# Exponentials of the first softmax transposed on VectorE, and the product with v in 32x32 tiles

## The chip, the cores and the metric

The kernel runs on one core of one Trainium2 chip. Its time is the device time of one execution in microseconds, given as the median of several executions. A core has TensorE (PE, with PEld for the loads of its stationary operand, the "weights"), VectorE (DVE), ScalarE (ACT), GpSimd (POOL), which here mostly issues loads, and SyncE (SP), which issues the output transfers. Each engine works through its own list of instructions in order; they wait for each other by semaphores.

## What is computed

Batch 8, 8 heads, 576 positions, head size 64, 32 packed rows. Two attentions follow each other, then a layer of two matrices with a squared ReLU between:

```python
def sm_attn(qq, kk, vv):
    s = scale * np.matmul(qq, kk.transpose(0, 1, 3, 2))
    s = s - np.max(s, axis=-1, keepdims=True)
    a = np.exp(s)
    a = a / (np.sum(a, axis=-1, keepdims=True) + 1e-09)
    return np.matmul(a, vv)
p_packed = sm_attn(p, k, v)              # 32 rows per head over 576 keys
out = sm_attn(q, p_packed, p_packed)     # 576 rows per head over 32 keys
x = out.transpose(0, 2, 1, 3).reshape(8 * 576, 512)
result = np.maximum(x @ w_in, 0) ** 2 @ w_out     # w_in 512x2048, w_out 2048x512
```

## The kernel before

Work is cut by batch b (0 to 7) and by quad qd (two groups of four heads). Four heads of 32 packed rows fill the 128 partitions.

For each batch and quad: k (and q) are loaded by POOL with a cast to bf16 as 128 rows of 18 positions x 64 (`load_rows`, L265 to L272; for batches 2 to 7, `WIDE`, in two halves of positions, and turned by some multiples of 32 partitions, which makes two transfers of one) and transposed in 32x32 blocks by VectorE into kT (`st_k`, L353). `st_s1` makes the first scores on PE in 32x32 tiles (`scores`, L377): four heads on four rows and columns of tiles, each head's 64 dimensions as two steps e. VectorE takes the negated maximum (L403), ScalarE the exponentials e1 with their sums (L415). Then e1 has to be turned so that keys lie on partitions: `st_e1T` (L435) does it on PE, in 128x128 transposes into PSUM, five a quad in batches 2 to 7 and six 96-row ones in batches 0 and 1 (`THREES`, whose scores are cut in thirds), and `st_e1T_out` copies the result to SBUF on VectorE or ScalarE (L421, L423). `st_pv` (L459) multiplies by v: 5 or 6 steps of keys, four heads in four column tiles, 64 columns each. v is loaded for it in another layout than k, `load_v` (L310, L315, L316), keys 4 or 6 in a row. Results are scaled by the reciprocal of the sums (L446, L472), transposed in two ways (ppd by VectorE, L480; ppT by PE, L498), and ppd is shifted by 64 partitions (`st_shift`) for the second attention.

The second attention: scores s2 (L377), transposed by VectorE (L517, L520), maximum, subtraction, exponentials, sums, normalization (L525 to L551) and transposition to a2T (L565). The first layer is folded into the packed rows: wp = ppT x w_in (L576, "w" words, copied out by "W" words), and h = wp x a2T (L592), relu (L597, L599), square into gT (L635, L637), and the second layer o (L650), which is copied out and sent by SP (L681).

The order is written out by hand: `ORDER` is a string of words, each a step, which are issued in that order; every engine gets its instructions in the order of the words. A word names a step, batch, quad or blocks, and after a colon the engine (v VectorE, a ScalarE, p POOL). `Lk00` loads k of batch 0 quad 0, `LA0`/`LB0` two parts of q of batch 0, `Wi11` a part of w_in, `Wo0` a part of w_out; `s100` scores, `m100` maximum, `x100` exponentials, `eT00` transposes, `eo00` their copy, `rd`, `pv`, `pp`, `bd`, `bs`, `pt`, `po` the steps around the product with v; `zA`, `tA`, `mA`, `sA`, `xA`, `uA`, `aA`, `TA` (and B) the second softmax of batches 0 and 1 in two parts of positions, `s2`, `t2`, ... `aT` that of the later ones; `h`, `r`, `q`, `o`, `c`, `d` the layers; `Z30` thirty dummy matmuls (`busy`, L337), which keep PE running while it waits at the start. `p_first` and `p_cast` load and turn p of batches 0 and 1; `Pr`, `Px`, `Pt`, `Pu` do it for the others, `Pu` being a copy of pT turned by 64 partitions, for the second half of the scores.

Of the kernel before, what the change touches and what calls it, by code (L numbers as in the profile page):

```python
# [29 lines left out]
THREES = range(2)  # L30
# [8 lines left out]
THIRDS = ((0, S // 3), (S // 3, S // 3 * 2), (S // 3 * 2, S))  # L39
# [11 lines left out]
pf Lk00 Lk01 Lv00 LA0 Lv01 Wi11 P0 Wi10 kT00 I Z30 s100 Wi00 LB0 kT01 P1 Wi01 m100 Z7 s101 Wi21 x100 m101 x101 Z6 eT00  # L51
Wi20 qA01 Z1 eT01 qA00 eo00:a eo01:v Lk10 rd0 Z5 pv0 pp0 bd0 Z3 pt0 Lk11 zA0 po0:v tA01 tA00 Z10 wb00 mA01 Wb00:a mA00
Z2 wb01 sA01:p Wb01:v Wo0 sA00:v xA01 uA01 xA00 Lv11 qB00 qB01 aA01:p uA00 Z21 zB0 Lv10 tB01 Z1 wa00 tB00 aA00:p mB01
Wa00:a Z1 wa01 TA01 mB00 Wa01:a sB01:p TA00 sB00:v Z5 h0.0.8 xB01 h0.0.1 xB00 r0.0.8:v h0.0.0 Wo2 r0.0.1:a h0.0.3 uB01
r0.0.0:a h0.0.10 uB00 h0.0.11 aB01:p r0.0.10:a h0.0.2 r0.0.3:a q0.0.0:v r0.0.2:a h0.0.9 r0.0.11:v aB00:p q0.0.1:a TB01
w101 LA1 q0.0.5:v r0.0.9:a w100 TB00 W101:a W100:v h0.1.0 q0.0.4:p h0.1.1 h0.1.11 r0.1.0:a h0.1.10 r0.1.1:a kT10
h0.1.2 r0.1.10:a LB1 h0.1.3 r0.1.11:a h0.0.12 r0.1.2:a q0.1.0:v h0.1.15 r0.1.3:a q0.1.5:p h0.0.4 r0.0.12:v r0.1.15:a
h0.0.13 kT11 r0.0.4:a h0.1.6 h0.0.5 r0.0.13:a Wo1 h0.0.6 q0.1.1:v r0.1.6:a h0.1.13 q0.0.6:v r0.0.5:a s11 r0.1.13:v Wo3
q0.0.2:a r0.0.6:v h0.1.14 m110 h0.1.7 r0.1.14:a h0.1.12 Pr h0.1.9 r0.1.7:a h0.1.4 q0.1.7:v r0.1.12:a h0.0.15 r0.1.9:v
x110 h0.0.14 r0.1.4:v h0.0.7 m111 r0.0.15:a h0.1.8 eT10 r0.0.14:a r0.1.8:v h0.1.5 r0.0.7:a o2.0 eo10:v q0.1.3:a o3.0  # L60
r0.1.5:v x111 q0.0.3:v o1.0 q0.1.2:v o0.0 q0.1.4:a q0.0.7:v o0.1 rd1 q0.1.6:p eT11 o1.1 eo11:v o3.1 pv1 Lk20 o0.2 pp1
o1.2 bd1 o3.2 o1.3 qA10 pt1 qA11 o0.3 o3.3 po1:v zA1 qB11 w011 tA11 o2.1 W011:a tA10 o2.2 qB10 o2.3 mA11 mA10 w110
w111 sA11 o3.4 Lk21 W110:a sA10 o1.4 W111:v o0.4 xA11 o0.5 xA10 uA11 zB1 w010 tB11 o1.5 uA10 o1.6 aA11 W010:a o0.6
mB11 o1.7 aA10 o2.4 Px TA11 Lk30 c1:v o3.5 o0.7 TA10 sB11 o3.6 kT20 d1 c0:a h1.0.8 Lv20 o2.5 r1.0.8:a Pt h1.0.3 xB11
h1.0.6 tB10 d0 r1.0.3:a o2.6 Pu:v h1.0.1 r1.0.6:a Lv21 o2.7 r1.0.1:a kT21 h1.0.0 c2:a h1.0.2 o3.7 r1.0.0:a uB11 Lv30
d2 r1.0.2:a s12 q1.0.0:v c3:a h1.0.4 mB10 o4.0 m120 q1.0.1:a Lq2 h1.0.5 d3 o5.0 r1.0.4:a m121 r1.0.5:a o5.1 aB11 x120
h1.0.12 q1.0.2:v h1.0.7 o4.1 kT30 Lq3 x121 eT20 o4.2 TB11 r1.0.12:a r1.0.7:v o5.2 sB10 eo20:a h1.0.13 rd2 q1.0.3:v
eT21 xB10 r1.0.13:v h1.0.9 eo21:a o4.3 r1.0.9:v h1.0.15 q1.0.6:a uB10 pv2 q1.0.4:v h1.0.10 pp2 o5.3 Lv31 r1.0.15:a
r1.0.10:v o4.4 aB10 pt2 h1.0.14 bd2 h1.0.11 po2:v r1.0.14:a o5.4 bs2:v r1.0.11:a w121 TB10 w020 q1.0.5:v W121:a h1.1.8
q1.0.7:v h1.1.9 o4.5 W020:v o5.5 r1.1.8:a r1.1.9:a o4.6 Lv40 h1.1.4 qT21 h1.1.6 r1.1.4:a o5.6 q1.1.4:a qT20 o4.7 Lk31  # L70
r1.1.6:a h1.1.2 o5.7 c4:v h1.1.14 r1.1.2:a s22 c5:a r1.1.14:v h1.1.10 t221 o6.0 d5 r1.1.10:a h1.1.1 t220 o6.1 r1.1.1:a
h1.1.7 m221 o6.2 d4 h1.1.0 r1.1.7:a o6.3 qT30 r1.1.0:a h1.1.5 q1.1.3:a h1.1.3 q1.1.0:v Lq4 o6.4 qT31 r1.1.5:a o6.5
q1.1.2:a sb21:v h1.1.13 r1.1.3:a o8.0 m220 r1.1.13:a h1.1.11 o6.6 q1.1.1:a Lq5 r1.1.11:v o6.7 x221 sb20:v h1.1.15 o8.1
c6:a q1.1.5:v h1.1.12 x220 su21 d6 o7.0 r1.1.12:a Lk41 w120 r1.1.15:a w021 kT31 q1.1.6:a o7.1 q1.1.7:a o8.2 su20
W120:a o7.2 o8.3 a221 W021:a o7.3 a220 o8.4 o7.4 aT21 o8.5 aT20 o7.5 h2.0.2 h2.0.3 r2.0.2:v o7.6 Lk40 r2.0.3:a o8.6
q2.0.1 o7.7 h2.0.1 h2.0.0 r2.0.1:v o8.7 r2.0.0:a c7:v s13 c8:a q2.0.0 h2.0.7 d7 h2.0.6 m130 Lk50 r2.0.7:a o9.0
r2.0.6:a h2.0.4 m131 o10.0 d8 r2.0.4:a h2.0.9 q2.0.3 x131 h2.0.5 r2.0.9:v o10.1 r2.0.5:v x130 o9.1 kT41 h2.0.12
h2.0.10 r2.0.12:a q2.0.2 eT31 Lk51 r2.0.10:a eT30 rd3 h2.1.1 eo31:v h2.0.8 r2.1.1:a o9.2 kT40 r2.0.8:a h2.1.0 eo30:a
o9.3 r2.1.0:v h2.0.11 Lk60 q2.0.4 pv3 q2.1.0 r2.0.11:a h2.1.3 pp3 o10.2 r2.1.3:a q2.0.5 h2.0.13 bd3 o10.3 bs3:v
r2.0.13:a Lv41 h2.1.5 h2.0.14 r2.1.5:v s23 q2.0.6 o9.4 qT40 r2.0.14:a h2.0.15 o9.5 t231 r2.0.15:a h2.1.4 h2.1.8 q2.0.7  # L80
o10.4 Lv51 r2.1.8:a t230 o9.6 r2.1.4:a o10.5 m231 h2.1.7 h2.1.2 q2.1.2 o9.7 r2.1.7:a qT41 r2.1.2:a o10.6 c9:a sb31:v
h2.1.11 Lq6 h2.1.14 r2.1.11:a d9 o11.0 q2.1.1 h2.1.6 m230 r2.1.14:a o11.1 r2.1.6:a o10.7 x231 sb30:v h2.1.10 h2.1.12
q2.1.3 pt3 r2.1.10:a o11.2 c10:v po3:a h2.1.9 r2.1.12:a su31 w030 x230 w130 d10 o11.3 r2.1.9:a q2.1.5 W030:a o12.0
q2.1.4 h2.1.13 su30 o12.1 W130:a o11.4 a231 o12.2 r2.1.13:a w131 a230 w031 o12.3 W031:a aT31 o11.5 aT30 h2.1.15 W131:v
o12.4 r2.1.15:a h3.0.0 h3.0.11 r3.0.0:a o12.5 q2.1.6 q2.1.7 r3.0.11:a h3.0.1 s14 r3.0.1:v h3.0.3 kT51 h3.0.7 r3.0.3:a
o11.6 r3.0.7:a m140 h3.0.10 o11.7 r3.0.10:a q3.0.0 h3.0.8 x140 kT50 h3.0.2 o12.6 r3.0.8:a c11:v o12.7 Lk61 r3.0.2:a
h3.0.14 q3.0.5 h3.0.5 d11 m141 o14.0 r3.0.14:a c12:a eT40 q3.0.1 h3.0.4 r3.0.5:a o13.0 x141 r3.0.4:v Lk71 h3.1.9 d12
eo40:v o14.1 r3.1.9:a q3.0.2 o13.1 h3.0.12 rd4 h3.0.6 o13.2 r3.0.12:v r3.0.6:a o14.2 h3.0.13 q3.0.3 h3.1.8 eT41
r3.0.13:v o13.3 r3.1.8:a eo41:v h3.0.9 q3.0.6 h3.0.15 o14.3 q3.1.4 r3.0.9:a r3.0.15:v pv4 q3.0.4 h3.1.5 Lv50 pp4
h3.1.6 r3.1.5:a q3.0.7 o14.4 bd4 o13.4 bs4:v r3.1.6:a pt4 Lv60 o14.5 h3.1.1 h3.1.0 po4:v r3.1.1:a o14.6 r3.1.0:v  # L90
h3.1.14 q3.1.0 w041 r3.1.14:a w141 o14.7 W141:v h3.1.3 W041:a h3.1.2 o13.5 o13.6 r3.1.2:a r3.1.3:v c14:a s24 q3.1.1
h3.1.7 h3.1.4 t240 r3.1.7:a o15.0 d14 r3.1.4:a o13.7 t241 h3.1.10 c13:a o15.1 q3.1.3 r3.1.10:a h3.1.12 q3.1.2 o17.0
m240 r3.1.12:a o17.1 d13 m241 h3.1.11 h3.1.13 r3.1.11:a o15.2 sb40:v r3.1.13:a h3.1.15 o15.3 q3.1.5 r3.1.15:a sb41:v
o17.2 x240 o17.3 q3.1.7 o15.4 x241 q3.1.6 su40 w140 w040 o15.5 W040:a su41 o17.4 o15.6 W140:a a240 o17.5 o15.7 a241
s15 c15:a aT40 o17.6 aT41 o16.0 m150 d15 h4.0.4 h4.0.10 kT60 r4.0.4:a o16.1 r4.0.10:a h4.0.0 m151 x150 o17.7 Lk70
h4.0.1 r4.0.0:v o16.2 x151 qT50 o16.3 r4.0.1:a h4.0.3 c17:v eT50 r4.0.3:a h4.0.2 q4.0.0 eo50:a o16.4 d17 r4.0.2:v
h4.0.7 rd5 qT51 o18.0 r4.0.7:a h4.0.11 q4.0.1 o16.5 Lq7 r4.0.11:a kT61 h4.0.6 h4.0.5 o18.1 r4.0.6:a q4.0.5 o16.6
r4.0.5:a q4.0.3 h4.0.13 q4.0.2 h4.0.12 r4.0.13:v eT51 o16.7 eo51:v r4.0.12:a h4.0.15 o18.2 q4.0.6 r4.0.15:a h4.0.9
# [38 lines left out]
class Kernel:  # L137
# [39 lines left out]
    def setup(self):  # L177
# [14 lines left out]
        for x in self.v_b:  # L192
            nc.vector.memset(x[:P // 2, :, 4, :], 0.0)
# [36 lines left out]
    def p_cast(self, b):  # L230

        g = slice(b * self.NQ, b * self.NQ + self.NQ)
        self.nc.vector.tensor_scalar_mul(self.p_b[:, g, :], self.p_f[:, g, :], SCALE)
        self.p_turn(g.start, g.stop)
# [590 lines left out]
```

## Time and profile before

| what | value |
|---|---|
| time, median of 3 executions | 243.79 us (243.75 to 244.76) |
| the profiled execution | 244.4 us, of which its span 242.6 us |
| busy: PE, DVE, ACT, POOL | 235.6, 205.7, 138.3, 76.0 us |
| second layer, L650 | 576 matmuls, 149.0 us busy |
| first layer, L592 | 512 matmuls, 89.6 us busy |
| transposes of e1, L435 | 84, of 219 and 220 ns each |
| copies of e1T | 9 on VectorE (484 and 538 ns), 7 on ScalarE (701 and 782 ns) |
| product with v, L459 | 336 matmuls of 64 columns, 195 ns each |
| dummy matmuls, L337 | 92, 15.9 us busy |
| first matmul of L592, last matmul | start 22.48 us, end 239.3 us |

The span is the time from the first to the last instruction of the program on the core; the execution's own time is 1.8 us more. A PE row's duration is that of one matmul from start to end; matmuls overlap, so what PE has to do for one is the distance from its start to the next one's. "128*32" in a PE row is the tile of the array in use, rows times columns. Idle time of an engine counts only where PE waits for it.

### The profile page before, as it was taken

What the parts mean: (1) busy time and instruction counts of PE and PEld (TensorE: products, weight loads), DVE (VectorE), ACT (ScalarE), POOL (GpSimd) and SP (SyncE); (2) the same over time, 40 slices, a digit from 0 to 9 for tenths busy, and PEclk for the clock granted to TensorE, in tenths of its full rate; (3) what the DMA queues carried; (4) which work ended last, traced back from release to release, by engine and by line L of the source; (5) the groups of instructions that cost most, each with busy time, mean ns of one, the idle gap of its engine ahead of it and who ended that gap; (6) DMA issues with size and microseconds to landing.
All of it is one profiled execution on the core that took longest, in us unless ns stands there. A gap on an engine that the chain in (4) does not pass through costs nothing.

```text
span 242.6 us, 6171 instructions
## 1 busy us (share of the span) xinstructions
PE 235.6 (97%) x2448; PEld 129.9 (54%) x2448; DVE 205.7 (85%) x455; ACT 138.3 (57%) x310; POOL 76.0 (31%) x125
## 2 busy tenths in 40 slices
PE   8999899999999999999999999999999999999994
PEld 5655564346554565456554664456544655555543
DVE  2679996999999899998899988997999899976830
ACT  2315981678687666865566645865584569523300
POOL 8647973792575484042400540002000000000000
PEclk9999999999999999999999999999999999999999
DMA  6999999999999899827841797125031210211214
GB/s 112 182 199 207 204 206 202 157 142 260 200 175 220 151 183 133 166 28 160 95 92 42 115 163 103 43 46 90 6 86 44 48 46 21 68 43 43 50 41 128
DMA packets 33404, 28.51 MB, mean 118 GB/s; under 512 B 8160, under 2 KB 28384, under 8 KB 33376
## 3 DMA queue, kind: packets, MB, share of 16 engines
q0 software_dynamic: 26848, 18.55, 53.8%
q1 hardware_dynamic: 6384, 9.51, 14.9%
q8 instruction: 19, 0.31, 0.5%
q10 hardware_dynamic: 144, 0.07, 0.1%
q14 instruction: 9, 0.07, 0.1%
HBM read 37.22 MB, written 9.44 MB: 192 GB/s over the span
## 4 chain that ended last, share of the span: by engine, by line
PE 83%; DMA 5%; POOL 3%; DVE 3%; issue 2%; ACT 1%; SPq 1%; POOLq 0%; ACTq 0%
PE ps_o L650 50%; PE ps_h L592 25%; DMA w_in_bf<-in_moe_w_in_dram 4%; PE ps_wp L576 3%; PE ps_s L377 2%; PE ps_e1T L435 2%; PE ps_pv L459 1%; POOL gT L310 1%; ACT r L597 1%; DMA out_dram<-o_sb 1%; DVE gT L637 1%; SPq L681 1%; DVE r L599 1%; POOL a L551 1%; POOL k_b L270 1%
## 5 line engine op out<-in xcount | busy, mean ns | idle before, releaser
L650 PE MATMUL ps_o<-w_out_bf,gT 128*128 128x512 bf16 (+1 forms) x576 | 149.0, 378 | 0.0
L597 ACT ACTIVATE r<-ps_h 128x288 bf16<-128x288 f32 (+2 forms) x181 | 68.9, 412 | 55.3 <-PE ps_h L592 54.8
L592 PE MATMUL ps_h<-a2T,wp 128*128 128x288 bf16 (+2 forms) x512 | 89.6, 286 | 1.4 <-DVE a2T L565 0.6
L650 PEld LDWEIGHTS <-gT 128*128 128x128 bf16 x576 | 54.3, 98 | 42.1 <-issue 4.0
L592 PEld LDWEIGHTS <-wp 128*128 128x128 bf16 x512 | 48.1, 98 | 42.4 <-issue 6.7
L637 DVE TENSOR_TENSOR gT<-r 128x576 bf16<-128x576 bf16 (+2 forms) x113 | 48.2, 447 | 3.0 <-ACT r L597 2.6
L599 DVE TENSOR_SCALAR r<-ps_h 128x288 bf16<-128x288 f32 (+2 forms) x75 | 33.2, 453 | 11.5 <-PE ps_h L592 10.3
L421 ACT CAST wp<-ps_wp 128x1024 bf16<-128x1024 f32 (+1 forms) x24 | 22.6, 962 | 16.5 <-PE ps_wp L576 16.3
L270 POOL DMA_DIRECT2D k_b<-in_k_dram x28 | 15.2, 545 | 37.5 <-DVE kT L353 25.5
L315 POOL DMA_DIRECT2D v_b<-in_v_dram x12 | 9.4, 787 | 33.4 <-PE ps_pv L459 29.6
L421 ACT COPY o_sb<-ps_o 128x512 f32<-128x512 f32 x22 | 12.9, 587 | 8.3 <-PE ps_o L650 8.2
L337 PE MATMUL ps_idle<-gT 128*128 128x288 bf16 x92 | 15.9, 325 | 1.1 <-DVE gT L189 1.1
L415 ACT ACTIVATE e<-ps_s,nm 128x576 bf16<-128x576 f32 x16 | 11.9, 750 | 7.8 <-DVE nm L403 7.7
L353 DVE STREAM_TRANSPOSE kT<-k_b 128x576 uint32<-128x576 uint32 x16 | 12.3, 771 | 3.0 <-DMA k_b<-in_k_dram 2.9
L270 POOL DMA_DIRECT2D q_b<-in_q_dram x16 | 11.0, 693 | 8.2 <-DVE qT L365 6.6
L365 DVE STREAM_TRANSPOSE qT<-q_b 128x576 uint32<-128x576 uint32 (+2 forms) x20 | 12.4, 637 | 1.1 <-DMA q_b<-in_q_dram 0.8
L423 DVE CAST wp<-ps_wp 128x1024 bf16<-128x1024 f32 (+1 forms) x10 | 11.7, 1166 | 1.0 <-PE ps_wp L576 0.9
L337 PEld LDWEIGHTS <-gT 128*128 128x128 bf16 x92 | 9.5, 110 | 5.6 <-DVE gT L189 1.1
L543 DVE TENSOR_REDUCE sums<-e 128x18 f32<-128x576 f32 (+2 forms) x20 | 12.2, 611 | 0.0
L537 ACT ACTIVATE e<-d 128x576 f32<-128x576 f32 (+2 forms) x20 | 11.4, 586 | 1.4 <-POOL d L531 1.2
L403 DVE TENSOR_REDUCE nm<-ps_s 128x1 f32<-128x576 f32 x16 | 11.5, 736 | 0.7 <-PE ps_s L377 0.7
L525 DVE TENSOR_REDUCE mx<-s 128x18 f32<-128x576 f32 (+2 forms) x20 | 11.9, 612 | 0.0
(60 smaller groups left out, 191.6 us busy)
## 6 DMA issues: line engine op xcount, KB each, us to landing
out_dram<-o_sb SPq DMA_DIRECT2D x65, 128.0 KB, 2.9
v_b<-in_v_dram POOLq DMA_DIRECT2D x12, 256.0 KB, 5.6
w_out_bf<-in_moe_w_out_dram POOLq DMA_DIRECT2D x4, 512.0 KB, 12.6
q_b<-in_q_dram POOLq DMA_DIRECT2D x6, 288.0 KB, 7.3
q_b<-in_q_dram POOLq DMA_DIRECT2D x12, 144.0 KB, 8.0
k_b<-in_k_dram POOLq DMA_DIRECT2D x12, 108.0 KB, 3.9
gT<-in_v_dram POOLq DMA_DIRECT2D x4, 288.0 KB, 10.9
w_in_bf<-in_moe_w_in_dram POOLq DMA_DIRECT2D x4, 256.0 KB, 10.9
```

The costliest lines, as they stand in the source:

```text
L270: engine.dma_start(x[n:], s[:P - n])
L337: self.nc.tensor.matmul(ps[:, :HALF], lhsT=self.nought[:, :P], rhs=self.nought, start=True, stop=True)
L353: self.nc.vector.transpose(t["kT"][:].rearrange("p s e -> p (s e)").bitcast(U32), t["k"][:].rearrange("p t d -> p (t d)").bitcast(U32))
L365: self.nc.vector.transpose(out.bitcast(U32), x.bitcast(U32))
L415: self.nc.scalar.activation(out, x, ACT.Exp, bias=t["nm"], accum_out=self.den[b][:, qd:qd + 1])
L421: engine.copy(out, x)
L543: nc.vector.reduce_sum(out=sums[:, x], in_=t["e2"][:, x], axis=AX.X)
L592: self.nc.tensor.matmul(ps, lhsT=t["wp"][:, fb // n, fb % n * P:(fb % n + 1) * P], rhs=t["a2T"][:, s0:s1], start=(qd == 0), stop=(qd == se ...
L597: engine.activation(r, ps, ACT.Relu)
L599: engine.tensor_scalar_max(r, ps, 0.0)
L637: engine.tensor_tensor(out=out, in0=r, in1=r, op=ALU.mult)
L650: self.nc.tensor.matmul(self.o[tt][:, e], lhsT=self.gT[:, fb, a:a + P], rhs=self.w_out_bf[:, fb, e], start=(i == 0), stop=(i == self.NFB - 1))
```

## The change

- The first scores of batches 0 and 1 are cut in halves like the others (`THREES` and `THIRDS` go).
- `st_exp1` writes e1 as (9 blocks, 32 positions, 2 halves) in all batches, and `st_e1T` is one VectorE transpose of 32x32 blocks of 4-byte pairs, 128x288, from SBUF to SBUF. `st_e1T_out` and its words `eo` go.
- v is loaded with `load_rows` in k's layout: 128 rows of 18 positions x 64. Quad 1 of batches 1 to 7 is turned by 64 partitions (`moved`), in two transfers.
- `st_pv` takes 18 steps of 32 keys with four heads in 32x32 tiles: 144 matmuls a batch.
- With the quads' heads on other partitions, k of quad 1 isn't turned any more, the scores' output columns are; the reciprocals of quad 1 are taken in halves from the other 64 partitions (three instructions, not one, in batches 1 to 7).
- The second copy of pT is turned by 32 partitions, not 64, and made by two SP transfers, not two VectorE copies. p of batches 0 and 1 is loaded by one transfer and cast in one piece, p of the others by one transfer.
- `ORDER` is new as a whole. The three memsets of v's buffers go.

```diff
-pf Lk00 Lk01 Lv00 LA0 Lv01 Wi11 P0 Wi10 kT00 I Z30 s100 Wi00 LB0 kT01 P1 Wi01 m100 Z7 s101 Wi21 x100 m101 x101 Z6 eT00
-Wi20 qA01 Z1 eT01 qA00 eo00:a eo01:v Lk10 rd0 Z5 pv0 pp0 bd0 Z3 pt0 Lk11 zA0 po0:v tA01 tA00 Z10 wb00 mA01 Wb00:a mA00
-Z2 wb01 sA01:p Wb01:v Wo0 sA00:v xA01 uA01 xA00 Lv11 qB00 qB01 aA01:p uA00 Z21 zB0 Lv10 tB01 Z1 wa00 tB00 aA00:p mB01
-Wa00:a Z1 wa01 TA01 mB00 Wa01:a sB01:p TA00 sB00:v Z5 h0.0.8 xB01 h0.0.1 xB00 r0.0.8:v h0.0.0 Wo2 r0.0.1:a h0.0.3 uB01
+pf Lk00 Lk01 I Lv01 Lv00 P0 LA0 Wi10 Wi01 kT00 LB0 Wi11 kT01 Z34 s100 Wi00 m100 s101 Wi20 x100 m101 x101 eT00 Wi21
+eT01 rd0 Z18 pv0 pp0 Lk10 qA00 bd0 qA01 Z7 pt0 po0:v Lk11 zA0 tA01 tA00 mA01 Wo0 mA00 sA01:v sA00:v Lv10 xA01 qB01
+uA01 xA00 qB00 aA01:p uA00 Z31 zB0 wb00 Lv11 tB01 Wb00:a tB00 aA00:v Z3 wb01 mB00 mB01 Wb01:a Z1 wa01 sB00:p TA00
+Wa01:a TA01 Z1 wa00 sB01:p h0.0.10 xB00 Wa00:v h0.0.11 r0.0.10:a h0.0.3 xB01 uB00 h0.0.2 h0.0.0 r0.0.11:a Wo2 uB01
...
-        self.v_b = [self.consts.tile([P, QH, 5, D], BF16, name=f"v_b{i}") for i in range(3)]
-        for x in self.v_b:
-            nc.vector.memset(x[:P // 2, :, 4, :], 0.0)
+        self.v_b = [self.consts.tile([P, T, D], BF16, name=f"v_b{i}") for i in range(3)]
...
-            self.copy(engine, z[P // 2:], y[:P // 2])
-            self.copy(engine, z[:P // 2], y[P // 2:])
+            self.load_rows(z, y, 1, self.nc.sync)
...
     def load_v(self, t, s, b, qd):
...
+        t["v"] = x
+        self.load_rows(x, s.rearrange("h (l t) d -> (h l) t d", t=T), self.moved(b, qd))
+
+    def moved(self, b, qd):
+
+        return 2 * qd if b else 0
...
     def st_exp1(self, t, b, qd):
...
+        out = e1[:].rearrange("p (j l a) -> p j l a", j=TURN, a=2)
+        x = t["ps_s1"][:, :, :HALF].rearrange("p a (j l) -> p j l a", l=NP)
...
-        for j, y in enumerate(x):
-            self.nc.tensor.transpose(ps[:, j, :], y, self.ident)
-        t["ps_e1T"] = ps
-
-    def st_e1T_out(self, t, engine):
-        ps = t["ps_e1T"]
-        t["e1T"] = self.tp.tile([P, T // 3, P], BF16, name="e1T")[:ps.shape[0], :ps.shape[1], :]
-        self.copy(engine, t["e1T"], ps)
+    def st_e1T(self, t):
+
+        x = t["e1T"] = self.tp.tile([P, TURN, NP, 2], BF16, name="e1T")
+        self.nc.vector.transpose(x[:].rearrange("p j r a -> p (j r a)").bitcast(U32), t["e1"][:].bitcast(U32))
...
+        self.nc.vector.reciprocal(x[:, :1], y[:, :1])
+        self.nc.vector.reciprocal(x[:n, 1:], y[n:, 1:])
+        self.nc.vector.reciprocal(x[n:, 1:], y[:n, 1:])
...
     def st_pv(self, b, *qds):
...
             for h in range(QH):
-                g = NP * h
-                self.nc.tensor.matmul(ps[g:g + NP, i, :D], lhsT=t["e1T"][:, j, g:g + NP],
-                                      rhs=t["v"][j][:, h, :], start=(j == 0), stop=(j == m[-1]))
+                r = (h + self.moved(b, qd)) % QH
+                r, c = slice(NP * r, NP * r + NP), slice(NP * h, NP * h + NP)
+                self.nc.tensor.matmul(ps[c, qd, :D], lhsT=t["e1T"][r, j % TURN, :, j // TURN], rhs=t["v"][r, j, :],
+                                      start=(j == 0), stop=(j == T - 1))
```

## The prediction

> **What bounds the kernel now.** I read the page's busy table and slices first, then the stretches (busy time of each engine per window), then the timeline around one batch, then the loads of TensorE weights (PEld) close up.
>
> ```profile
> PE 235.6 (97%) x2448; PEld 129.9 (54%) x2448; DVE 205.7 (85%) x455; ACT 138.3 (57%) x310; POOL 76.0 (31%) x125
> ...
> PE 83%; DMA 5%; POOL 3%; DVE 3%; issue 2%; ACT 1%; SPq 1%; POOLq 0%; ACTq 0%
> ```
>
> ```profile
> 22.50:34.10 11.60, 10.56 (x134) 7.18 (x134) 11.07 (x26) 11.13 (x31) 9.75 (x13) 1.00 1.24 207
> ...
> 80.00:105.00 25.00, 25.00 (x300) 13.52 (x305) 23.87 (x51) 17.59 (x40) 10.40 (x18) 1.00 0.87 143
> 105.00:130.00 25.00, 25.00 (x274) 13.48 (x249) 22.58 (x49) 15.59 (x35) 6.84 (x12) 1.00 0.54 91
> ```
>
> The columns after the window are its length and the busy time of PE, PEld, DVE, ACT and POOL, then clock and DMA. From about 34 us to 239.3 us (last matmul) PE is full; VectorE has 1.1 to 2.4 us left in 25. A busy PE hides waits, so I compared, from 34.1 us on, the distance between starts of the full-width matmuls with their columns' time (a 288-column one comes every 122 ns, a 512-column one every 216). Only 1.2 us in all of it is waiting; each of 36 entries into small-tile matmuls costs another 94 ns. So in this part the time moves with what PE has to do, hardly with anything else. Before it lies a prologue: the first layer-1 matmul starts at 22.48 us, behind loads and the softmax chain of batch 0, while PE fills with dummy matmuls.
>
> ```profile
> 85.30 0.72 PE L435 MATMUL ps_e1T<-ident,e 128*128 128x128 bf16 x10
> 85.86 0.65 PE L592 MATMUL ps_h<-a2T,wp 128*128 128x288 bf16 x4
> ...
> 87.84 0.49 PE L459 MATMUL ps_pv<-v_b,e1T 128*32 128x64 bf16 x40
> 88.26 0.42 PE L592 MATMUL ps_h<-a2T,wp 128*128 128x288 bf16 x2
> ```
>
> Start to next start: ten transposes hold PE 0.558 us (56 ns each, though a row's duration is 219), the product with v 0.421 us (exactly, from the trace's starts). That is 0.979 us a batch in batches 2 to 7. In batch 1 it is twelve transposes, 0.333 and 0.335 us, and 48 matmuls in 0.486: 1.154 us.
>
> **PE: transposes out, product in smaller tiles.** The program's order of instructions has 84 transposes less and 1152 product matmuls in place of 336: 144 a batch (18 steps x 4 heads x 2 quads), each with its own weight load. No row shows so long a run of small tiles, so the rate must come from short ones.
>
> ```profile
> 81.42 0.19 PEld L377 LDWEIGHTS <-pT 32*32 32x32 bf16 x32 [0.42 <-issue]
> ...
> 37.78 0.21 PEld L459 LDWEIGHTS <-e1T 96*32 96x32 bf16 x15
> ```
>
> The first row (scores, 32x32 tiles) is 32 loads in 0.19 us; less the last one's own 0.09 us, one per 3.3 ns. The second is the tail of the 48-pair product of batch 1: 15 loads in 0.21 us, less 0.09, over 14 distances: 8.4 ns. In the single starts, every run longer than some 32 pairs goes over to 8 and 9 ns, in 32x32 tiles (scores of batch 1) and 128x32 ones alike; the first of that cadence stands about 0.215 us behind the run's start, when the first matmul (193 ns) is done. I read this as 32 pairs ready in advance and then a feed of 8.3 ns a pair, whatever the tile. So 144 pairs: 0.215 + 111 x 8.3 ns = 1.14, and 0.13 us from the last load to the next full-width matmul (59.700 to 59.834): **1.28 us**. Bounds: at 3.3 ns throughout, 144 x 3.3 + 0.13 = 0.61; at the old product's whole mean, 421/40 = 10.5 ns, 1.51. I take 1.28, since the 8.3 ns is the row of the longest runs.
>
> Batches 2 to 7: 1.28 - 0.979 = +0.30 each, +1.8. Batch 1: 1.28 - 1.154 = +0.13. Its first scores change from 48 matmuls of 192 columns (0.636 us, 30.21 to 30.85) to 32 of 288, which take 0.41 in later batches: -0.22. Entries into small tiles: as many as before (36), nothing. Sum **+1.7 us**, bounds -3.0 (6 x -0.37, -0.54, -0.22) and +3.3 (6 x 0.53 + 0.36 - 0.22).
>
> Two rules of the Trainium skill bear on this. "TensorE: Matmul & The Clock Gate", Part 4, puts a transpose in a kernel at about 275 ns; by it the removed ones would be 84 x 0.275 = 23 us of PE; the starts say 56 ns each, so the trace differs, and 4.7 us stand. Part 3 of the same page prices packed tiles at one matmul's duration plus about 4 ns a tile; that is 0.193 + 143 x 0.004 = 0.77 us a product, and it is the second rival below; the trace agrees for 32 pairs and not beyond.
>
> **VectorE and ScalarE.** Added on VectorE: 16 transposes of e, 128x288 uint32, 447 ns in the row of a2T with the same shape, and in seven batches two more reciprocals of 150 ns; removed: 9 copies of e1T (484 and 538 ns), 3 memsets, 2 copies of pT. With the changed split of r, q, c and W between the engines, counts times row means give VectorE +3.4 us and ScalarE -3.3 (7 copies of e1T gone). Per late batch the step itself is 2 x 0.447 + 2 x 0.15 - 0.484 (one of its two copies stood on VectorE) = +0.71 us, in a batch of 25 us in which VectorE has at least 1.1 idle. Cost nothing, hidden under full PE; the cover leaves some 0.4 us. The exponentials are written contiguously as before and keep their 750 ns.
>
> **DMA, POOL, SP.** v comes as 128 rows of 2304 bytes instead of pieces of 768, 512 and 128 bytes. In the prologue k's 288 KB took 1.41 us from landing to landing, v's 2.47 and 1.69: taking 1.41 for v saves 1.3 us before the second w_in pair. The bounds are nothing and 1.4. In the full part nothing waits for v's landing: nothing. The turned copy of pT becomes two SP transfers, behind only output DMAs; output rows land in 2.9 us, and batch 2's scores, the first reader, come over 5 us later: nothing; if late, one wait of up to 3 us. Behind them on SP stand output transfers, for whose rows five buffers are there. p's first 128 KB come in one transfer, not three, and land before k's first: nothing. The identity's two POOL instructions (0.55 us) move ahead of v's loads; the transfers of k run until 7.24 us anyway: nothing.
>
> **The prologue, walked through in the new order.** Each POOL load is issued when the one eight before it has landed. Dummies: 34 rather than 30, +4 x 122 ns, scores 100 from 7.9; the second max ends at 10.05 (10.52 before), the second exp at 11.0, its VectorE transpose at 11.5, the product 11.5 to 12.75 (13.31 before). Then q's first transposes, which before stood in the shadow of the copies, come behind pp: scores zA at 14.45 (14.21). LB0 moves one place up, with leaner v in front: it lands at about 16 rather than 18.9, so POOL's a of quad 1 goes at 18.7, not 19.9. But both subtractions and a of quad 0 now stand on VectorE, and its row there (transposes .92, maxima .84, subtractions .97, q .8, sums 1.4, transposes .8, a .44, maxima .77, a2T .67) runs without a break from 14.7 to about 22.6. So the VectorE chain takes the place of the loads: first layer-1 matmul 22.6 (22.48), second half's a2T ready 26.0 (26.34). I take **0**, with 1.3 us either way.
>
> Sum: +1.7 + 0 + 0. The profiled execution (244.4, span 242.6) would become 246.1; the shown median is 0.6 under it, 243.79 + 1.7 = **245.5**.
>
> **Rivals.**
> 1. Forecast: the feed of 8.3 ns a pair prices the product, 245.5, about 244.2 to 246.8 with the prologue's play. Chance 0.52.
> 2. Not slower: the long run keeps the burst's rate, as eight 32x32 tiles are free in turn and nothing is held. At 3.3 ns: 243.8 - 3.0 = 240.8. It decides when a product takes under 1.04 us, where 6 x (x - 0.979) + x - 1.154 - 0.22 is nothing. For it speaks the x32 row; against it, all longer runs. Chance 0.14. By the Trainium skill's 4 ns a tile (the page above, Part 3) it would be 6 x -0.21 - 0.38 - 0.22 = -1.9, so 241.9.
> 3. The prologue gains what v's leaner loads save, 1.3 us, because VectorE's chain is packed tighter than I walked it: 245.5 - 1.3 = 244.2. Against it, that chain has no loads in it after 16 us. Chance 0.17.
> 4. VectorE becomes the bound: where the order bunches its work, the 0.71 us a batch exceed the cover, and PE waits for r or q. At half of 6 x 0.71, +2.1: 247.6. It decides where VectorE passes some 98% of a stretch. Chance 0.14.
> 5. Tiles don't overlap at all: four 64-column matmuls took 29 ns on four tiles, so one at a time would be 144 x 29 = 4.2 us, +3.2 x 7: 266. The 32 scores in 0.41 us speak against it. Chance 0.02. That the change doesn't do what it says has 0.01: the instruction counts show it.
>
> Range: leaving out most of rival 2 and part of 4, 242.3 to 247.6. A measurement here tells 0.5%, 1.2 us, from no change. Faster by that (under 242.6): rival 2 and a little of 3, 0.16. Within it (to 245.0): most of 3 and the lower part of the forecast, 0.29. Slower: 0.55.
>
> **What would show it.** In the new profile: the product's 144 matmuls 1.2 to 1.3 us from first start to the next full-width one, weight loads 8 to 9 ns apart after about the thirty-second; e1T transposes near 447 ns on VectorE; first layer-1 matmul between 21.9 and 23.3; VectorE 208 to 210 us busy; waits in the full part still 1 to 2 us. A product of 0.8 us or less makes the sum wrong, and so does a full part with over 3 us of waits.

## The result, and the profile after

The changed kernel takes **258.46 us** (median of four executions, 258.14 to 259.89) beside 244.26 for the kernel before on the same chip (243.75 to 244.76): a ratio of 1.059, interval 1.054 to 1.064. The forecast was 245.5, the range ended at 247.6. It went to the side with the largest chance, but eight times as far. Times here are medians of all executions of a kernel; the ratios leave out the few executions that ran over 1.5% longer than the fastest of their kernel, at a lower granted clock.

The page of the changed kernel, in part (busy times; the TensorE clock; the instruction queue; the chain; the first group):

```profile
PE 240.6 (93%) x3118; PEld 132.8 (51%) x3151; DVE 208.5 (81%) x467; ACT 134.7 (52%) x306; POOL 64.0 (25%) x110
...
PEclk9977999689999999999999999999999999999999
...
q8 instruction: 24, 0.39, 0.6%
...
PE 73%; DVE 15%; issue 6%; DMA 2%; ACT 2%; POOL 0%; DVEq 0%; POOLq 0%
...
L625 PE MATMUL ps_o<-w_out_bf,gT 128*128 128x512 bf16 (+1 forms) x543 | 143.9, 382 | 6.2 <-issue 4.6
```

PE is busy for 5 us more, but the span is 15.5 us longer (258.1 against 242.6), so PE's share falls from 97% to 93%. "Issue" in the chain grows from 2% to 6%: time in which PE waits for nothing that the profile knows. Two stretches of the clock row, slices 3 and 4 and slices 8 and 9, are below 9; before has a 9 throughout. VectorE's 208.5 us lie in the forecast 208 to 210; it is not the bound.

Where this time lies, the timeline of PE shows at the products (L434) of batch 0 and batch 1:

```profile
11.80 1.20 PEld L434 LDWEIGHTS <-e1T 32*32 32x32 bf16 x140 [0.24 <-DVE rden L420]
11.80 1.30 PE L434 MATMUL ps_pv<-gT,e1T 32*32 32x64 bf16 x139
...
17.22 0.26 PE L434 MATMUL ps_pv<-gT,e1T 32*32 32x64 bf16 x5 [4.11 <-issue]
17.22 0.11 PEld L434 LDWEIGHTS <-e1T 32*32 32x32 bf16 x4 [4.22 <-issue]
```

```profile
41.81 1.24 PEld L434 LDWEIGHTS <-e1T 32*32 32x32 bf16 x144 [0.42 <-DVE e1T L413]
41.81 1.35 PE L434 MATMUL ps_pv<-gT,e1T 32*32 32x64 bf16 x144
...
43.08 0.11 PEld L625 LDWEIGHTS <-gT 128*128 128x128 bf16 x2
...
43.31 0.38 PE L625 MATMUL ps_o<-w_out_bf,gT 128*128 128x512 bf16 x1 [0.16 <-issue]
...
47.64 0.13 PEld L625 LDWEIGHTS <-gT 128*128 128x128 bf16 x2 [4.45 <-issue]
47.65 1.04 PE L625 MATMUL ps_o<-w_out_bf,gT 128*128 128x512 bf16 x2 [3.96 <-issue]
```

The product of batch 0 stops for 4.1 us with four pairs left to load; the four go on afterwards with no releaser. The loads of batch 1's product run through in 1.3 us (41.81 to 43.08), as forecast, and two matmuls later PE stands still for 4.0 us. A third pause of 0.7 us is in batch 7 (205.02 to 205.73). Together 8.8 us. After the second one the windows show what it leaves behind (length; busy time of PE, PEld, DVE, ACT, POOL; clock; DMA share; GB/s):

```profile
44.00:48.00 4.00, 0.35 (x1) 0.13 (x2) 0.00 (x0) 0.00 (x0) 2.09 (x5) 0.82 1.29 204
48.00:50.00 2.00, 2.00 (x8) 0.82 (x6) 0.29 (x1) 0.00 (x0) 2.00 (x5) 0.50 1.17 207
50.00:52.00 2.00, 2.00 (x20) 0.36 (x19) 0.77 (x1) 0.32 (x1) 1.61 (x3) 0.50 1.15 192
52.00:54.00 2.00, 2.00 (x8) 0.73 (x6) 1.92 (x5) 0.69 (x1) 0.00 (x0) 0.65 1.01 169
54.00:56.00 2.00, 1.84 (x37) 0.59 (x36) 0.86 (x2) 1.01 (x1) 0.00 (x0) 1.00 1.18 197
```

From 48 to 54 us PE is "busy" in every window at a granted clock of 0.50, 0.50 and 0.65: 1.0 + 1.0 + 0.7 = 2.7 us of work lost that no idle time shows. The pause of batch 0 has the same tail (0.50 from 17 to 21 us), in a stretch in which PE waits anyway; with it, the first layer-1 matmul starts at 27.83 us (22.48 before).

**What stands at the pauses.** Queue q8 brings instructions: 24 packets, 0.39 MB, so 16 KB each (19 in the kernel before). Counted along PE's own list, a pair being two instructions, the pauses in the changed kernel fall at 256 times 2, 5 and 22, if 64 instructions are taken to stand ahead of the kernel's first one. (The 64 are chosen so that the first pause falls on 512; the other two then come within 6 instructions of their multiples.) So I read: PE's instructions come in blocks of 256; two blocks are there; the packet with the next one is fetched once a block has been used up. The trace's records of the first packets of the changed kernel (times in us):

```
block used up at  its successor's packet starts (lasts)  next block used up at  pause
   256:  11.86        14.76 (0.96)                          512:  12.92          4.1, resumes 17.22
   512:  12.92        20.79 (0.91)                          768:  29.98          -
  1024:  41.87        45.26 (0.95)                         1280:  43.31          4.0, resumes 47.64
  1280:  47.64        49.78 (0.95)                         1536:  65.54          -
```

(The pause at 512 lies at its end, so the packet at 20.79 comes 3.6 us after PE resumed.) From "used up" to "resumes" it takes 5.4 and 5.8 us: 2.9 and 3.4 until the packet starts, 0.95 of packet, 1.5 and 1.4 after it. A product of 288 instructions at 8.3 ns a pair uses up a whole block in 1.1 us. A layer-2 matmul of 512 columns takes 216 ns for its two instructions, so that a block of those lasts nearly 28 us. In the kernel before no block of 256 is used up in less than 7.9 us, and none comes late. That is **Theory A**, the supply of instructions. In the runs below, too, every pause of over 0.3 us that shows no releaser lies at such a count: 32 in all profiles together, and behind each the weight loads go on 1.2 to 1.7 us after the end of the packet that was missing. The rivals of Theory A: the run of 32x32 tiles itself brings the pauses, or the new order of steps does.

### The profile page after: what moved, and what is told of

Read it like the earlier page. It is cut to its first block, busy times and chain, and to the rows that moved or that the text cites. A ratio compares the mean times of both kernels' runs of the same rounds, so it can differ in the third digit from the quotient of the medians.

```text
span 258.1 us, 7525 instructions
## 1 busy us (share of the span) xinstructions
PE 240.6 (93%) x3118; PEld 132.8 (51%) x3151; DVE 208.5 (81%) x467; ACT 134.7 (52%) x306; POOL 64.0 (25%) x110
## 4 chain that ended last, share of the span: by engine, by line
PE 73%; DVE 15%; issue 6%; DMA 2%; ACT 2%; POOL 0%; DVEq 0%; POOLq 0%
PE ps_o L625 38%; PE ps_h L567 21%; PE ps_pv L434 4%; PE ps_idle L328 4%; PE ps_wp L551 3%; PE ps_s L368 3%; DMA k_b<-in_k_dram 2%; DVE gT L612 2%; DVE mx L500 1%; DVE d L506 1%; DVE r L574 1%; ACT r L572 1%; DVE kT L344 1%; DVE sums L518 1%; DVE nm L392 1%
## 5 line engine op out<-in xcount | busy, mean ns | idle before, releaser
L625 PE MATMUL ps_o<-w_out_bf,gT 128*128 128x512 bf16 (+1 forms) x543 | 143.9, 382 | 6.2 <-issue 4.6
L572 ACT ACTIVATE r<-ps_h 128x288 bf16<-128x288 f32 (+2 forms) x178 | 67.4, 413 | 56.1 <-PE ps_h L567 55.4
L625 PEld LDWEIGHTS <-gT 128*128 128x128 bf16 x576 | 55.4, 99 | 48.0 <-issue 8.8
L612 DVE TENSOR_TENSOR gT<-r 128x576 bf16<-128x576 bf16 (+2 forms) x107 | 45.5, 445 | 1.6 <-ACT r L572 0.8
L406 ACT CAST wp<-ps_wp 128x1024 bf16<-128x1024 f32 (+1 forms) x22 | 20.8, 956 | 18.2 <-PE ps_wp L551 17.9
L261 POOL DMA_DIRECT2D k_b<-in_k_dram x28 | 15.5, 556 | 44.8 <-DVE kT L344 27.3
L328 PE MATMUL ps_idle<-gT 128*128 128x288 bf16 x95 | 17.1, 346 | 1.1 <-DVE gT L187 1.1
L408 DVE CAST wp<-ps_wp 128x1024 bf16<-128x1024 f32 (+1 forms) x12 | 14.1, 1173 | 3.1 <-PE ps_wp L551 3.0
L261 POOL DMA_DIRECT2D v_b<-in_v_dram x12 | 6.8, 567 | 35.0 <-PE ps_pv L434 35.0
L434 PEld LDWEIGHTS <-e1T 32*32 32x32 bf16 x1152 | 10.1, 88 | 8.4 <-issue 5.7
L328 PEld LDWEIGHTS <-gT 128*128 128x128 bf16 x95 | 10.6, 116 | 6.7 <-DVE gT L187 1.1
L447 DVE TENSOR_TENSOR pp<-ps_pv,rden 128x256 bf16<-128x256 f32 x8 | 3.4, 420 | 10.8 <-PE ps_pv L434 10.8
```

Source lines behind the costliest of these rows:

```text
L261: engine.dma_start(x[n:], s[:P - n])
L328: self.nc.tensor.matmul(ps[:, :HALF], lhsT=self.nought[:, :P], rhs=self.nought, start=True, stop=True)
L406: engine.copy(out, x)
L408: engine.tensor_copy(out, x)
L434: self.nc.tensor.matmul(ps[c, qd, :D], lhsT=t["e1T"][r, j % TURN, :, j // TURN], rhs=t["v"][r, j, :], start=(j == 0), stop=(j == T - 1))
L572: engine.activation(r, ps, ACT.Relu)
```

## The experiments

All ratios are to the kernel before on the same chip.

**e1_shift**: only the cut of the first dummy matmuls differs, so that all block ends move by 128 instructions.

```diff
-    def busy(self, n):
+    def busy(self, n, m=HALF):        # and [:, :m] in its matmul
- ... kT01 Z34 s100 ...
+ ... kT01 Z98x100 s100 ...
```

> The changed kernel, with its first 34 dummy matmuls of 288 columns made 98 of 100, so that PE has 128 instructions more before the first product and about the same dummy time; nothing else. Theory A (code supply: PE's instructions arrive in blocks of 256, of which two are there; a product of 288 instructions that meets a block's end in its first tens of instructions, or just before them, uses up the next block before another has come; in the changed kernel that happened in batches 0, 1 and 7): the pauses without a wait of 4.3 us in batches 0 and 1 and 0.8 us in batch 7 go, since a block's end now lies 151, 165 and 125 instructions into their products; new ones appear in batch 2 (3 before the product), batch 4 and batch 6 (33 into it), between 0.8 and 4 us each. Time 252 to 258 us. Theory B (the pauses belong to these products, by their data, PSUM or the loads that run beside them): they stay in batches 0, 1 and 7, and the time stays at 258. Theory C (the new order and VectorE's longer chain make the loss, the pauses are small beside it): the time stays within 3 us of 258.

260.34 us, ratio 1.064 (1.059 to 1.068). The pauses moved: batch 7 lost its own, batches 0 and 1 kept 0.5 us each, and batches 2, 3, 4 and 6 got 1.6, 1.9, 3.0 and 1.7 us. One of them, in PE's timeline:

```profile
119.24 1.23 PEld L434 LDWEIGHTS <-e1T 32*32 32x32 bf16 x144 [0.24 <-issue]
119.24 1.34 PE L434 MATMUL ps_pv<-v_b,e1T 32*32 32x64 bf16 x143
...
123.56 0.18 PE L434 MATMUL ps_pv<-v_b,e1T 32*32 32x64 bf16 x1 [2.98 <-issue]
```

A product that ran through in the changed kernel stops here at its last matmul, though nothing near it was edited. The pauses belong to the count of instructions. The sum did not fall, since other products now lay badly: the time lies above the 252 to 258 us of Theory A and by itself would fit its rivals, so it is the places of the pauses that speak here.

**e2_aligned**: the dummies recut so that block ends lie less badly (Z83x118, Z5x403, Z18x496; 98 instructions more, then 30 fewer).

> The changed kernel, dummies recut (83 of 118 columns, 5 of 403, 18 of 496 for 34, 7 and 31 of 288) so that block ends lie 181, 225, 57, 113, 93, 137, 93 and 185 instructions into the eight products. Theory A: at most a pause of 1 to 2 us in batch 1 (block end 31 instructions before its product, loads full) and under 1 us in batch 2; none elsewhere; no stretch at half clock after 45 us; time 245 to 249 us, which is the change without its pauses. Theory B: pauses as before, 258. Theory C: within 3 us of 258, with VectorE behind PE's waits.

252.11 us, ratio 1.030 (1.025 to 1.034), granted clock 1.00, first layer-1 matmul at 22.40. So 6.3 us of the 14 go by the cut of dummy matmuls alone; it stayed 3 us above what I expected, since pauses of 1.4, 1.0, 1.9, 0.4 and 0.2 us were left, 4.9 in all.

**e3_half**: the product takes 9 of its 18 steps, so half of the keys are left out of p_packed.

```diff
-        for j, qd in [(j, qd) for j in range(T) for qd in qds] ...
+        for j, qd in [(j, qd) for j in range(T // 2) for qd in qds] ...
```

> The changed kernel with half of the product: 9 of the 18 steps of keys, 72 matmuls a batch (half of the keys are left out of the packed rows). 144 instructions cannot hold two block ends. Theory A: no pause over 1.5 us; a product costs 0.68 us from its start to the next full-width matmul (0.215 + 39 x 8.3 ns + 0.13); time 242 to 245. Theory B: pauses in batches 0, 1 and 7 remain. Theory C: 252 or more, since VectorE's work and the order are all there.

244.34 us, ratio 0.995 (0.991 to 0.999). No pause over 0.25 us; products of 72 pairs take 0.68 us where nothing else holds them (0.215 + 39 x 8.3 ns + 0.13 gives 0.67). New is a wait of 1.9 us at 54.1 us, where the scores of batch 2 wait for the turned copy of pT that SP transfers (the profile is of the longest of ten executions, 246.04 us, so I take only the kind of this wait from it).

**e4_before_long**: the kernel *before*, with its transposes on TensorE and its order, but its own product done over so that it has 144 matmuls a batch.

```diff
-        for j, i in ...:
+        again = ...
+        for x, (j, i) in enumerate((again * 4)[-36:]):
+            extra = x < 36 - len(again)
-                    start=(j == 0), stop=(j == m[-1]))
+                    start=(extra or j == 0), stop=(extra or j == m[-1]))
```

> The kernel before, its own product in 128x32 tiles issued over and over until it has 144 matmuls a batch; only the last pass counts, the others are overwritten. Transposes on PE, v's layout, VectorE's work and the order stay. Theory A: the instruction count alone makes pauses: block ends lie 11, 3 and 9 instructions from the start of the products of batches 2, 6 and 7, and 17 to 29 before those of 3, 4 and 5, so pauses of 0.5 to 4 us there; products of about 1.28 us for 0.42 give +6; time 251 to 257. Theory B: no pause, 250. Theory C: as before plus 6 at most, 250, no pause.

259.1 us, ratio 1.059 (1.055 to 1.063), the same as the change. Its product in batch 2, with 128x32 tiles:

```profile
61.75 1.15 PEld L461 LDWEIGHTS <-e1T 128*32 128x32 bf16 x133 [0.26 <-ACT e1T L421]
61.75 1.26 PE L461 MATMUL ps_pv<-v_b,e1T 128*32 128x64 bf16 x133
...
66.37 0.15 PEld L461 LDWEIGHTS <-e1T 128*32 128x32 bf16 x11 [3.47 <-issue]
```

It is 2 us above what I expected, with pauses of 1.2, 3.4 and 1.2 us, without 32x32 tiles in the product, without the VectorE transposes and in the old order: both rivals fall. That its time equals the change's is chance, since some 6 us of it were expected for the longer products.

**f1_split, f3_aligned_split, f4_all**: the products cut in two by quad, with other matmuls between (f1: the changed kernel; f3: e2_aligned; f4: f3 with the late loads of f2_late_loads below).

```diff
- pv2 r1.0.8:v h1.0.15 q1.0.4:v h1.0.12 pp2 ...
+ pv20 r1.0.8:v h1.0.15 q1.0.4:v h1.0.12 r1.0.15:a o5.4 ... pv21 ... pp2 ...
```

> The changed kernel with its products of batches 1 to 7 cut in two by quad: 72 pairs of one quad, then 1.3 to 3 us of layer-1 and layer-2 matmuls, then 72 pairs of the other. The steps that follow each product move back with the second half; the number of TensorE instructions and their places in the blocks of 256 stay. Theory A (instructions come in blocks of 256, and a pause is what is missing when 256 of them are used up before the next block has come): the pause of batch 0, whose product stays whole, remains 4.3 us; the pause of batch 1 shrinks by what stands between the halves, from 4.3 to about 2.1 us, and the half clock behind it goes with it; that of batch 7 goes from 0.9 to about 0.3. Each batch pays 0.15 us for a second entry into small tiles. Sum 258.5 - 2.2 - 3 - 0.6 + 1 = 253.7 us (252 to 256). Rival (the pauses belong to the number of small-tile pairs, or to the places of the block ends alone): pauses of 4.3, 4.3 and 0.9 us as before, 259 us.

> e2_aligned with its products cut in two by quad as in f1_split. Theory A: of the pauses of e2_aligned (1.35 in batch 0, 1.0, 1.9, 0.4, 0.25 us) the first stays, batch 2's falls to about 1 us, the others go; seven second entries and short runs cost 0.15 us each: 252.1 - 2.6 + 1 = 250.5 us (249 to 252). Rival (as in f1_split): pauses as in e2_aligned, 253 us.

> f3_aligned_split with the late loads of f2_late_loads as well. Theory A: as f3_aligned_split, since batch 1 has no pause left there, or 0.5 us less where a block of this stretch came late: 250 us (248.5 to 252). If the later loads are late for what reads them, a wait with a DMA as releaser shows between 50 and 60 us, and the time is over 252. It is the version of the change with the least pauses; by the sum of the prediction (+1.7 us of TensorE work) it should not pass below 244.5.

273.45, 270.31 and 271.06 us: all three missed by some 20 us. The pauses did go: outside batch 0 (4.3, 1.2 and 1.7 us) none is over 0.25 us in f1 and f3, and one of 0.5 us is left in f4. But the edit made two new waits. The loads of a later batch's v, which stood behind the whole product, now overtake its second half and write into the buffer that it reads; so some second halves multiply by another batch's v (these three don't compute what the changed kernel does) and wait for it. f3, batch 4:

```profile
121.11 0.74 PE L413 MATMUL ps_pv<-v_b,e1T 32*32 32x64 bf16 x72
...
126.37 0.23 PE L413 MATMUL ps_pv<-v_b,e1T 32*32 32x64 bf16 x2 [3.05 <-DMA v_b<-in_v_dram]
...
127.41 1.14 PE L413 MATMUL ps_pv<-v_b,e1T 32*32 32x64 bf16 x70 [0.81 <-DMA v_b<-in_v_dram]
```

And the wp steps, moved back with the product, are waited for in most batches (1.4, 1.1, 0.8 us and more in f1). Half clock follows the longest of these stops (129.87 to 136.70 us in f1). These waits carry a releaser; the pauses of Theory A don't. The times say nothing about A, the absence of pauses speaks for it.

**f2_late_loads**: the changed kernel, its block ends unmoved, with the last quarter of w_out and k of batch 2 loaded only behind batch 1's product.

```diff
- ... s11 Wo3 q0.0.3:a ... q0.1.7:v Lk20 o1.0 ... pv1 o1.1 pp1 o2.1 ...
+ ... s11 q0.0.3:a ... q0.1.7:v o1.0 ... pv1 o1.1 pp1 Y Wo3 Lk20 o2.1 ...
```

(Y is the one-column copy of pp.)

> The changed kernel with whole products, but the last quarter of w_out and the loads of batch 2's k are issued only once pp of batch 1 is there (a one-column GpSimd copy of pp stands before them), so that the DMA engines are nearly empty while batch 1's product runs. The places of the block ends are the same. Theory A with its second half (the instruction packet waits behind data on full DMA engines): the packet behind boundary 1024 starts 0 to 1.5 us after the crossing, not 3.4; the pause of batch 1 is 0.9 to 2.4 us, not 4.3, and the half clock behind it goes: 253 us (251 to 255). If the packet's delay has nothing to do with the data transfers: 3.4 us, a pause of 4.3 us, half clock, 258.5 us. The pause of batch 0 remains 4.3 us by both.

256.51 us, ratio 1.052 (1.048 to 1.057). The same place, with a DMA share of 0.7 to 0.9 rather than 1.5:

```profile
41.44 1.35 PE L412 MATMUL ps_pv<-gT,e1T 32*32 32x64 bf16 x144
...
42.71 0.11 PEld L603 LDWEIGHTS <-gT 128*128 128x128 bf16 x2
...
42.95 0.38 PE L603 MATMUL ps_o<-w_out_bf,gT 128*128 128x512 bf16 x1 [0.16 <-issue]
...
45.20 0.11 PEld L603 LDWEIGHTS <-gT 128*128 128x128 bf16 x2 [2.37 <-issue]
```

The packet starts 1.2 us after the crossing (3.4 in the changed kernel) and the pause is 1.9 us, not 4.0. So here the data transfers hold the instruction packet up. Over all thirteen profiles, 138 blocks were used up with the DMA engines full (share of 0.9 or more over the 2 us about it) and got their packet 2.7 us later in the median; 117 with a share under 0.5 got it at about that moment. Half clock came all the same (46.08 to 49.50 us, some 1.7 us of work lost), and the time stays above the expected 251 to 255.

**g1_padded** and **g2_padded_shift**: e2_aligned with 208 TensorE instructions more that add no work (finer cuts), and the same kernel with one word changed.

```diff
 # g1, from e2_aligned
- ... kT01 Z83x118 s100 ...
+ ... kT01 Z109x90 s100 ...
+            cut = 2 if ... else 1     # 24 layer-1 and 54 layer-2 matmuls
+            for c in range(cut):      # in two column halves
 # g2, from g1
- ... kT01 Z109x90 s100 ...
+ ... kT01 Z173x57 s100 ...
```

> The changed kernel, whole products and its own order, with TensorE instructions added that cost no work, so that each product's block ends fall 125 to 233 instructions behind its start and the 256 that hold a product are used up slowly: the first dummies are cut 109 x 90 columns (9,810, as 34 x 288 were 9,792), the next 5 x 403 and 18 x 496; 24 layer-1 matmuls of batch 0, 32 layer-2 matmuls of the first four row tiles and 22 of the seventh and eighth are cut in two column halves. Theory A, stepped through block by block with the supply times of the earlier runs (5.3 us from crossing to resuming before 70 us, 4.2 before 125, 3.3 later): pauses of 0.8 us (2 at the slowest supply), all but 0.4 of it in batch 0. e2_aligned had 5.2 us of pauses and 252.1 us: so 247.7 us (247 to 249), which is the 245.5 of the prediction, 0.8 of pause and 1 us in which four products wait for VectorE's e1T. If the 14 us that the change lost have another cause than the supply of instructions: 252 us or more, since nothing else is better placed than in e2_aligned.

> g1_padded with one edit: the first dummies are cut 173 x 57 columns instead of 109 x 90, the same columns in 64 more instructions, so that every block end moves by 128 instructions and lies at the worst place again. Theory A, stepped through as for g1_padded: pauses of 0.7 and 4.1 us about batch 0, 3.7, 4.2, 2.8, 2.2, 0.2 and 2.2 us in the batches after it, 20 us in all (24 at the slowest supply): 267 to 272 us, and more by 2 to 3 us for each pause of over 4 us that brings half clock. If the places of the block ends don't matter: as g1_padded within 1 us, since the work is the same.

**248.76** us, ratio 1.019 (1.017 to 1.022), and **271.54**, ratio 1.115 (1.111 to 1.119). The same work, the same order, 9,810 and 9,861 columns of first dummies (the product of batch 0 starts at 11.29 and 11.76 us), and 23 us between them. Batch 1 of g1 and batch 3 of g2:

```profile
35.56 1.24 PEld L412 LDWEIGHTS <-e1T 32*32 32x32 bf16 x144 [0.42 <-DVE e1T L391]
35.56 1.35 PE L412 MATMUL ps_pv<-gT,e1T 32*32 32x64 bf16 x144
...
36.84 0.55 PEld L609 LDWEIGHTS <-gT 128*128 128x128 bf16 x4
36.84 1.04 PE L609 MATMUL ps_o<-w_out_bf,gT 128*128 128x512 bf16 x4
```

```profile
96.48 1.41 PEld L412 LDWEIGHTS <-e1T 32*32 32x32 bf16 x144 [0.42 <-DVE e1T L391]
96.48 1.51 PE L412 MATMUL ps_pv<-v_b,e1T 32*32 32x64 bf16 x143
...
101.64 0.20 PE L412 MATMUL ps_pv<-v_b,e1T 32*32 32x64 bf16 x1 [3.64 <-issue]
```

In g1 the next matmul starts 1.28 us after the product's start, the forecast's number, and pauses of 0.4 us are left in batch 0 and at 41.59 us (0.8 in all, as expected). In g2 there are seven pauses, 15.1 us in all (20 to 24 expected), and four stretches of half clock, 20.5 us long together. Both times lie in the ranges that Theory A gave from a step-through of the blocks; g2's number is partly luck, since its pauses came out 5 us shorter than stepped through and its half clock longer.

**g3_early_turn**: g1_padded with `Pr`, `Px`, `Pt` and `Pu`, which prepare pT for batches 2 to 7, earlier.

```diff
+ ... Pr Wo1 ...            # was behind r0.1.15:v
+ ... W010:a Px o3.2 ...    # was behind o0.6
+ ... qA10 Pt Pu o0.3 ...   # were behind o1.7 and TA11
```

> g1_padded with the preparation of pT for batches 2 to 7 moved ahead, on GpSimd (the load of p in front of the second quarter of w_out), on ScalarE and VectorE (the scaling and the transpose some 6 us earlier) and so on SP (its two transfers some 6 us earlier). Its trace showed TensorE waiting 2.3 and 1.9 us for these two transfers, which took 7.7 and 8.9 us to land; e2_aligned, which came 1.3 us later to this place, waited 0.3 us. Theory: this wait is the only large one left, so it goes and no pause takes its place: 248.8 - 2.5 = 246.3 us (245.3 to 247.3), about 0.8 over the prediction's 245.5, of which 1 us is four waits for e1T, 0.4 us the last pause, and -0.9 us the shorter prologue. If the wait only uncovers another (the next reader, a load of batch 2's k or q): 248 to 249 us. It should stay above the kernel before by 1 us or more.

247.93 us, ratio 1.014 (1.009 to 1.019), 0.6 above the expected bounds. The wait for the transfer is gone; in its place the second scores of batch 1 stand for 0.6 us. The profile names VectorE's pT transpose as releaser, but that ended at 42.21 us and the scores start at 42.58. The stop lies at a block end (1536), 1.46 us after the end of its packet, as the one of 0.4 us in g1_padded did; so it is the supply again, though VectorE's next transpose of q, which ends at 42.61, might have held the scores about as long. A pause of 0.25 us is back in batch 2. The wait of 3.6 us from which I had sized the gain stood in a profiled execution of g1_padded that took 253.15 us, beside 248.4 to 248.9 for the others. The gain is 0.8 us between the medians, and the intervals of the two ratios overlap. This is the best version of the change here, and it is still behind the kernel before. Its clock row and chain:

```profile
PE 239.1 (97%) x3289; PEld 139.5 (57%) x3289; DVE 208.9 (85%) x467; ACT 134.5 (55%) x306; POOL 64.0 (26%) x110
...
PEclk9999999999999999999999999999999999999999
...
PE 80%; DVE 14%; ACT 2%; issue 1%; DVEq 0%
```

With nearly all pauses gone, "issue" is at 1% (2% before the change) and PE back at 97%.

## Why the prediction was wrong

**The step that failed** is the sum "+1.7 + 0 + 0" in its assumption that PE, given 144 pairs, is limited only by the feed of 8.3 ns. The product's own time was right where nothing interrupts it. What the sum put at nothing is the supply: an engine that issues 288 instructions in 1.2 us uses up a block before the next one has come, and this wait was neither in the sum nor among the rivals, although the profile of before shows the queue (q8, 19 packets) and the instruction counts. Of the 14.2 us, 8.8 are pauses and 2.7 half clock after the second. The 2.7 left hold the forecast's 1.7 and 1.0 more; the half clock in the prologue no run took apart, the cost of the change with few of its pauses left is taken apart at the end of this section.

The Trainium skill, "Runtime: NRT & Kernel Launch", "Instruction fetch mechanics", describes refilling in blocks of 256 instructions, which the trace confirms, and calls the cost of a block's end mostly hidden. That held for every block of the kernel before, each of which lasted 7.9 us or more. Of the 23 blocks in these profiles that were used up in under 3 us, 21 ended in a pause of 0.7 us or more, and the trace's 4.1 us decide.

Point by point:

- *Product 1.28 us.* Right where nothing interrupts: 1.277 to 1.280 in batches 4 and 6 of the changed kernel, and batch 1 of g1. Loads lie 8 and 9 ns apart from the 34th on, 3 and 4 ns in the 32 first. The others without a pause took 1.43 to 1.62: in batch 2 the loads stop for 0.37 us for e1T, in batches 3 and 5 for 0.16 us; the cause of these, and of 0.22 us behind the product of batch 1, stays open. In g3_early_turn the products of batches 1 to 7 take 1.47 us on average, one pause included: the term was too small by 1.3 us in all.
- *Rival 2, the burst rate throughout, and rival 5, no overlap (4.2 us a product).* Shown wrong by the same loads.
- *Transposes of e1 on VectorE at 447 ns.* 433 to 480. *VectorE hidden.* Nearly: in the changed kernel PE stands idle for e1T once (batch 2, 0.17 us). The four products to which my later expectations gave 1 us of such waits take 0.8 us over 1.28 together in g1_padded.
- *Prologue 0, first layer-1 matmul at 22.6.* 22.40 in e2_aligned with 1.4 us of pause still in it; 21.57 in g1_padded with 0.4 and 21.83 in g3_early_turn with none. So there is a gain of 0.65 to 0.9 us, nearer to rival 3's 1.3 than to the forecast's nothing.
- *Batch 1's first scores, -0.22.* Not there: 0.636 us before, 0.633 in g3_early_turn. The 0.41 of the later batches did not carry over.
- *Transposes on PE, 56 ns.* Right, but the prediction set it beside another quantity: the 275 ns that it takes from the Trainium skill ("TensorE: Matmul & The Clock Gate", Part 4) are the duration of one transpose, to which the row's 219 ns belong, and not a distance between starts.
- *SP's two transfers of pT: nothing, or one wait of up to 3 us.* Hidden in the changed kernel, because the pauses made everything else late; a wait of 0.3 us in e2_aligned and of 1.3 us in e1_shift.
- *The waits in the full part still 1 to 2 us.* The place where the prediction said it would break: over 3 us makes the sum wrong, and there were 4.7 (4.0 and 0.7), beside the 4.1 of the prologue.

What the change costs with few of its pauses left is seen in g3_early_turn: 3.7 us over the kernel before, against 1.7 forecast. Added up by the distances from each matmul's start to the next, from the first layer-1 matmul on, the product less the transposes is +3.2 (+1.9 forecast), wp with the wait of 0.6 us behind it +0.5, layer 1 +0.3, layer 2 +0.1 (the 78 matmuls cut in two among them) and the scores +0.1 (-0.22 forecast): +4.2 in all. The prologue gives -0.65. That makes 3.5, the difference of the two spans (246.1 and 242.6). So beside the supply the term of the sum that was too small is the product.

## What to carry to other kernels

Count instructions as well as columns: before a long run of tiny matmuls is put into a full engine, divide the engine's list into blocks of 256 and look how long each lasts; here nearly all that lasted under 3 us ended in a pause, which the profile books as "issue" without a releaser, some of those from 3 to 5.6 us did, most of them in the first 70 us, while data transfers fill the DMA engines, and none that lasted longer did. A time that moves by several per cent when idle work is recut is a sign of it. And a stop of some 2 to 4 us can cost 1.7 to 3 us more in half clock behind it, so that a busy engine in the profile is not proof that nothing was lost.

## What the runs showed of the hardware

- The place of block ends alone moved one and the same work from 248.8 to 271.5 us.
- A block's packet takes 0.9 to 1.0 us in most cases and 2.0 at most. With the DMA engines full it starts 2.7 us, in the median, after the block before it is used up, and at about that moment when they are less than half used. PE goes on 1.2 to 1.7 us after the packet's end.
- Half clock followed pauses of 4.1, 4.0, 3.4 us and two of 1.9 and 1.7 us (0.50 at 184 to 186 us in e1_shift), but not one of 3.0 us (1.00 throughout behind 123.56 there) or 1.9 us (e2_aligned). Length alone doesn't decide it. The records of the clock show what does, save for one case: in every run the clock changes only on a grid of 3.41 us (half clock in the changed kernel starts at 15.84 and 46.56 us and lasts two steps, 6.83 us, each time). Up to the last matmul, half clock began behind 16 steps of this grid, in each of which PE's rows show it idle for 1.7 us or more, and behind none with 1.6 us or less. The pause of 3.0 us lay across two steps, with 1.5 us idle in the one and 1.6 in the other; the one of 1.7 us lay whole in one step. The exception is e2_aligned's, 1.9 us idle in one step (63.72 to 67.13) and no half clock.
- Two SP transfers of 128 rows within SBUF took 1.9 to 2.4 us to land in the changed kernel, 5.5 to 6.9 in e1_shift, e2_aligned and g3_early_turn, and 7.7 and 8.9 in g1_padded's profile, where two VectorE copies of before had taken 0.36 us each.
